# Order of the first loads, of the first two weight conversions and of the down-weight sums in a retention + SwiGLU kernel

## The chip, the cores and the metric

One core of one Trainium2 chip. The metric is the device time of one execution in microseconds, the median of several runs. A time is compared only with runs of the kernel before that were made on the same chip at the same time. Ratios are the mean time of one kernel's fast runs over that of the other's of the same rounds, so they are not quite the ratio of the medians quoted beside them.

The engines have short names in the profile: PE is TensorE, DVE is VectorE, ACT is ScalarE, POOL is GpSimd, SP is the engine that issues the loads.

## The reference

```python
# retention: B, H, S, D = 4, 8, 768, 64
for t in range(S):
    state = gamma * state + outer(k[:, :, t], v[:, :, t])
    y[:, :, t] = scale * (q[:, :, t] @ state)
# feed-forward: x is (3072, 512), d_ff = 1536; the three weights are 64-bit floats
g = x @ w_gate
out = (g * sigmoid(g) * (x @ w_val)) @ w_out
```

## The kernel before

The work goes in four segments of 768 tokens. Attention of a segment is done in six chunks of 128 positions, then twelve "up" blocks f = 0 to 11 compute the hidden activations, then a "down" stage multiplies by w_out, interleaved with the attention of the next segment. Up and down products use a scheme with seven products in place of eight, which needs sums of weights and sums of activations (`xs`, `hs`).

The first segment is special. The weights arrive as 64-bit words and are converted on the chip to 32-bit, piece by piece, while the blocks run. Twelve "up" pieces and six "down" pieces go through three steps and then their sums. The line numbers are those that the profile of the kernel before shows:

```python
def convert_a(piece):                                   # ScalarE, L172 and L173
    nc.scalar.activation(d, hi, AF.Abs)
    nc.scalar.activation(lo, lo, AF.Copy, scale=2.0 ** -51, bias=2.0)
def convert_b(piece):                                   # VectorE, L179 and L181
    nc.vector.tensor_scalar(d, d, ...min, max)
    nc.vector.tensor_scalar(hi, hi, 0x80000000, None, op0=ALU.bitwise_and)
def convert_c(piece):
    nc.vector.scalar_tensor_tensor(u, u, 3, hi, ...)    # VectorE, L188
    nc.gpsimd.tensor_tensor(d, u, lo, op=ALU.add)       # GpSimd, L190, "the add"
def sums_t(piece):                                      # L201 to L203
    sub = (nc.gpsimd if kind == "up" else nc.vector).tensor_tensor
    sub(both, ...); sub(w[:, T2], ...); sub(w[:, T4], ...)
```

An up block, with its calls into the conversion (cut):

```python
def up(s, f, convert):
    product(x, B11, a_up(0, 0));  nc.scalar.copy(p1, x)          # L359
    product(wb, T1, s1);          nc.scalar.copy(p5, wb)         # L362
    ...                                # Silu of the block before, ScalarE
    convert(f, 0)                      # b and c of the next-but-one pieces
    product(x, T2, s2, start=False);  nc.scalar.copy(u2, x)      # L368
    product(wb, B22, s4, start=False); tt(hT[:, f, 0], wb, u2)   # VectorE, L370
    product(x, T3, s3, start=False);   tt(hT[:, f, 1], x, p5)    # VectorE, L372
    ...                                # gate products of the block before, L389, L390
    convert(f, 1)
    product(z, B21, a_up(0, 1));       tt(c11, z, p1)            # VectorE, L380
    product(x, T4, a_up(1, 1), start=False)   # adds into x: must wait for L372
```

The traces show VectorE taking its instructions in program order: where the down sums (L201, at 111.67) wait 2.51 us for GpSimd, all that follows them waits too. The last product adds into `x`, which L372 has to read first; so whatever stands before L372 in VectorE's order can hold up TensorE.

Of the kernel before, what the change touches and what calls it, by code (L numbers as in the profile page):

```python
# [32 lines left out]
MASK0, QDEC0, KDEC0, GDEC0 = 0, 2 * NP * P, 3 * NP * P, 3 * NP * P + H  # L33
# [4 lines left out]
def tile_retnet_swiglu(  # L38
# [32 lines left out]
    nc = tc.nc  # L71
# [10 lines left out]
    first = early.__enter__()  # L82
# [4 lines left out]
    def bank(tag, bufs, name):  # L87
        return psum.tile([P, 512], F32, tag=tag, name=name, bufs=bufs)


    chunks = {}

    def load_chunk(c, pool, tag, between=lambda nm: None):
        tiles = []
        for nm, src in (("kt", k_t), ("qt", q_t), ("vn", v_n), ("kn", k_n)):
            t = pool.tile([P, 512], F32, tag=nm + tag, name=f"{nm}_{c}")
            nc.sync.dma_start(out=t, in_=src[c])
            tiles.append(t)
            between(nm)
        chunks[c] = tiles  # L100

    def seg_chunks(s):

        p, pos = divmod(s * L, NCK)
        return [(2 * p + i) * NCK + pos + j for j in range(L) for i in range(2)]

    tab = consts.tile([P, NTAB], F32, name="tab")
# [17 lines left out]
    def load_piece(piece):  # L125


        kind, a = piece
        to = new_wt(0, a) if kind == "up" else wot[a]
        if kind == "up":  # L130
            halves = [w[:, ts(a, P)].rearrange("(c p) f -> p c f", p=P)
                      for w in (w_gate, w_val)]
            parts = [(halves[1][:, ds(KH, KH)], B22), (halves[1][:, ds(0, KH)], B12),
                     (halves[0], B11)]
        else:
            top, low = (w_out[ts(a + FH * i, P)] for i in range(2))
            parts = [(low[:, DH:], B22), (top[:, DH:], B12), (top[:, :DH], B11),
                     (low[:, :DH], B21)]
        if w_gate.dtype != F32:
            raw[piece] = raws.tile([P, 4, 2 * KH * P], U32, tag="raw",  # L140
                                   name=f"raw_{kind}{a}")
        for src, slot in parts:
            if w_gate.dtype == F32:
                t = to[:, slot:]
            else:
                t, src = raw[piece][:, slot - B22:], src.bitcast(U32)
            if len(src.shape) == 3:
                c, f = src.shape[1:]
                t = t.rearrange("p a b -> p (a b)")[:, : c * f]
                t = t.rearrange("p (c f) -> p c f", c=c)  # L150
            else:
                t = t[:, 0]
            nc.sync.dma_start(out=t, in_=src)
# [8 lines left out]
    def words_of(piece):  # L162
        kind, a = piece
        w = wt[0, a] if kind == "up" else wot[a]
        d = w[:, ds(B22, 4)].rearrange("p a b -> p (a b)")
        r = raw[piece].rearrange("p a (n two) -> p (a n) two", two=2)
        return w, d, r[:, :, 0], r[:, :, 1]

    def convert_a(piece):
        if piece in raw:  # L170
            w, d, lo, hi = words_of(piece)
            nc.scalar.activation(d, hi.bitcast(F32), AF.Abs)  # L172
            nc.scalar.activation(lo.bitcast(F32), lo, AF.Copy, scale=2.0 ** -51,  # L173
                                 bias=2.0)

    def convert_b(piece):
        if piece in raw:
            w, d, lo, hi = words_of(piece)
            nc.vector.tensor_scalar(d, d, 122879.9921875, 2.0 ** -15, op0=ALU.min,  # L179
                                    op1=ALU.max)  # L180
            nc.vector.tensor_scalar(hi, hi, 0x80000000, None, op0=ALU.bitwise_and)  # L181
# [12 lines left out]
    def sums_t(piece):  # L194
        kind, a = piece
        w = wt[0, a] if kind == "up" else wot[a]
        sub = (nc.gpsimd if kind == "up" else nc.vector).tensor_tensor
        flat = w.rearrange("p a b -> p (a b)")
        n = KH * P
        both = flat[:, : 4 * n].rearrange("p (a b) -> p a b", b=2 * n)[:, :, :n]  # L200
        sub(both, w[:, ds(B22, 2)], w[:, ds(B12, 2)], op=ALU.subtract)  # L201
        sub(w[:, T2], w[:, B22], w[:, T1], op=ALU.subtract)
        sub(w[:, T4], w[:, B21], w[:, T2], op=ALU.subtract)  # L203
        if kind == "up":
            nc.sync.dma_start(out=wstore[a], in_=w)
# [8 lines left out]
    def load_next():  # L214
        if to_load:
            load_piece(to_load.pop(0))
# [107 lines left out]
    def a_up(i, j):  # L324
        return xT[:, ds(KH * j, KH), i]
# [13 lines left out]
    late = []  # L339

    def up(s, f, convert):
        w = wt.pop((s, f)).rearrange("p o (k f) -> p o k f", k=KH)
        s1, s2, s3, s4 = xs
        x = bank("x", 2, f"x_{s}_{f}")[:, :TH]
        wb = bank("wz", 2, f"w_{s}_{f}")[:, :TH]

        def product(o, slot, a, start=True, stop=True):
            for k in range(KH):
                nc.tensor.matmul(o, w[:, slot, k], a[:, k], start=(start and k == 0),  # L349
                                 stop=(stop and k == KH - 1), skip_group_check=True)  # L350

        def tmp(nm, bufs):
            return io.tile([P, TH], F32, tag=nm, name=f"{nm}_{s}_{f}", bufs=bufs)

        add, mul = ALU.add, ALU.mult
        tt = nc.vector.tensor_tensor
        product(x, B11, a_up(0, 0))
        p1 = tmp("p1", 2)
        nc.scalar.copy(p1, x)  # L359
        product(wb, T1, s1)  # L360
        p5 = tmp("p5", 1)
        nc.scalar.copy(p5, wb)  # L362
        if late:
            late[0]()
        convert(f, 0)
        product(x, T2, s2, start=False)
        u2 = tmp("u2", 1)
        nc.scalar.copy(u2, x)  # L368
        product(wb, B22, s4, start=False)
        tt(hT[:, f, 0], wb, u2, op=add)  # L370
        product(x, T3, s3, start=False)
        tt(hT[:, f, 1], x, p5, op=add)  # L372
        if late:
            late.pop(0)
            late.pop(0)()
        convert(f, 1)
        z = bank("wz", 2, f"z_{s}_{f}")[:, :TH]
        product(z, B21, a_up(0, 1))
        c11 = tmp("c11", 2)
        tt(c11, z, p1, op=add)  # L380
        product(x, T4, a_up(1, 1), start=False)
        sg = tmp("sg", 1)

        def gates():
            nc.scalar.activation(c11, c11, AF.Silu)
            nc.scalar.activation(sg, x, AF.Silu)

        def muls():
            tt(hT[:, f, 0], hT[:, f, 0], c11, op=mul)  # L389
            tt(hT[:, f, 1], hT[:, f, 1], sg, op=mul)  # L390

        late.extend([gates, muls])
# [63 lines left out]
            nc.scalar.dma_start(out=out[ds(row, P)], in_=ev[i])  # L456


    def table(nm):
        if nm == "qt":  # L460
            nc.sync.dma_start(out=tab[:, :QDEC0], in_=decays[:, :QDEC0])
        elif nm == "vn":
            nc.sync.dma_start(out=tab[:, QDEC0:], in_=decays[:, QDEC0:])

    cs = seg_chunks(0)
    load_chunk(cs[0], first, "0", table)
    for n in range(1, len(cs)):
        load_chunk(cs[n], first, str(n))
        if n in (1, 3, 4):
            load_next()  # L470
    steps = retention(0)

    def retain(k):
        for _ in range(k):
            if steps:
                steps.pop(0)()

    u0, u1 = order[:2]
    retain(3)
    convert_a(u0)  # L480
    retain(3)
    convert_b(u0)
    retain(2)
    convert_c(u0)
    load_next()
    convert_a(u1)
    retain(3)
    convert_b(u1)
    retain(1)
    sums_t(u0)  # L490
    retain(4)
    convert_c(u1)
    load_next()
    retain(len(steps))
# [3 lines left out]
    due = [u1]  # L498
# [3 lines left out]
    def convert(f, part):  # L502
        now = at_block[f]
        if part == 0:
            while due:
                sums_t(due.pop(0))
            for p in now:
                convert_b(p)
            for p in now[:1]:
                convert_c(p)  # L510
                load_next()
                if p[0] == "up":
                    sums_t(p)
                else:
                    due.append(p)
        else:
            for p in now[1:]:
                convert_c(p)
                load_next()
                due.append(p)  # L520
            for p in at_block[f + 1] if f + 1 < NF else []:
                convert_a(p)

    for s in range(NSEG):
        nxt = seg_chunks(s + 1) if s + 1 < NSEG else []
# [70 lines left out]
```

## Time and profile before

| | before |
|---|---|
| median of 4 runs (range) | 795.73 us (794.53 to 796.8) |
| TensorE busy | 758.9 us, 96% |
| TensorE's largest wait | 13.9 us, for L372 on VectorE |
| two up blocks, first segment / later segments | 22.5 us / 18.06 us |

A line of a wait list reads: who waited, for whom, us in total, times, longest. A line of the order of time reads: start in us, duration in us, engine, line, operation, output<-inputs, form, and in brackets the idle time before it and what ended it. The lines themselves are shown in the prediction.

### The profile page before, as it was taken

Reading aid. Unit: us, or ns where it says so; the run is one execution under the profiler, and the core shown is the slowest. Engines: PE = TensorE matmul, PEld = TensorE weight load, DVE = VectorE, ACT = ScalarE, POOL = GpSimd, SP = SyncE. Lnnn points to the kernel's source line nnn. Section 1 sums busy time; section 2 is a strip of 40 time slices with the busy share of each in tenths; the row PEclk is TensorE's granted clock in tenths of the full one; section 3 lists DMA queues with packets and bytes.
Section 4 is the critical chain, followed back from the end, with each engine's and each line's share of the span. In section 5 each row is a group of like instructions: output and inputs, shape, how many; then the busy total and the mean of one; then the engine's idle time right before and its main releaser. Section 6 shows DMA issues by size and latency. Waiting matters only on the chain.

```text
span 794.6 us, 8792 instructions
## 1 busy us (share of the span) xinstructions
PE 758.9 (96%) x3440; PEld 532.4 (67%) x3440; DVE 333.4 (42%) x524; ACT 202.4 (25%) x422; POOL 138.2 (17%) x102
## 2 busy tenths in 40 slices
PE   5889888989999999999999999999999999999997
PEld 4755454557888555557888655556888755555886
DVE  2778888885241232225441322225433222223520
ACT  2374454411211222221122222322111122322100
POOL 3665766732110000100211000001211000000000
PEclk9899999999999999999999999999999999999999
DMA  9856667331550223500532223320254023310010
GB/s 328 287 199 232 203 220 250 148 120 54 186 195 31 93 92 99 192 0 28 199 118 108 73 93 113 128 97 14 67 212 159 27 93 113 119 47 0 1 54 26
DMA packets 40840, 95.73 MB, mean 120 GB/s; under 512 B 3680, under 2 KB 15968, under 8 KB 40800
## 3 DMA queue, kind: packets, MB, share of 16 engines
q1 hardware_dynamic: 37344, 88.89, 32.1%
q10 hardware_dynamic: 3456, 6.29, 2.3%
q8 instruction: 27, 0.44, 0.2%
q14 instruction: 13, 0.11, 0.0%
HBM read 77.86 MB, written 17.30 MB: 120 GB/s over the span
## 4 chain that ended last, share of the span: by engine, by line
PE 77%; DVE 3%; issue 0%; ACT 0%; DVEq 0%; ACTq 0%
PE x L349 24%; PE dx L417 15%; PE w L349 12%; PE dw L417 7%; PE z L349 6%; PE dz L417 4%; PE y L296 2%; PE s L246 2%; PE y L292 2%; PE st L274 2%; DVE hs L407 1%; DVE hT L390 0%; DVE a L251 0%; DVE hT L372 0%; DVE wot L201 0%
## 5 line engine op out<-in xcount | busy, mean ns | idle before, releaser
L349 PE MATMUL x<-xT,wt 128*128 128x384 f32 x384 | 136.3, 497 | 13.9 <-DVE hT L372 13.9
L349 PE MATMUL x<-xs,wt 128*128 128x384 f32 x384 | 139.8, 487 | 1.2 <-ACT u L368 1.2
L349 PE MATMUL w<-xs,wt 128*128 128x384 f32 x384 | 139.6, 486 | 0.9 <-DVE xs L334 0.9
L349 PEld LDWEIGHTS x<-xT,wt 128*128 128x128 f32 x384 | 73.8, 194 | 67.6 <-issue 20.8
L370 DVE TENSOR_TENSOR hT<-w,u 128x384 f32<-128x384 f32 x48 | 26.7, 557 | 214.0 <-PE w L349 213.1
L349 PEld LDWEIGHTS x<-xs,wt 128*128 128x128 f32 x384 | 72.7, 190 | 53.2 <-ACT u L368 3.3
L349 PEld LDWEIGHTS w<-xs,wt 128*128 128x128 f32 x384 | 73.0, 190 | 52.4 <-DVE xs L334 1.6
L257 POOL TENSOR_TENSOR kn<-kn,tab 128x512 f32<-128x512 f32 x20 | 25.2, 1261 | 330.4 <-DMA kn<-in_k_n_dram 330.4
L359 ACT COPY p<-x 128x384 f32<-128x384 f32 x48 | 23.0, 479 | 226.2 <-PE x L349 226.1
L349 PE MATMUL z<-xT,wt 128*128 128x384 f32 x192 | 69.8, 486 | 0.0
L417 PE MATMUL dw<-wot,hs 128*128 128x256 f32 x288 | 67.3, 383 | 0.0
L417 PE MATMUL dx<-wot,hs 128*128 128x256 f32 x288 | 67.0, 382 | 0.0
L417 PE MATMUL dx<-wot,hT 128*128 128x256 f32 x288 | 66.4, 381 | 0.0
L417 PEld LDWEIGHTS dw<-wot,hs 128*128 128x128 f32 x288 | 53.7, 190 | 8.7 <-issue 1.5
L417 PEld LDWEIGHTS dx<-wot,hT 128*128 128x128 f32 x288 | 53.7, 190 | 8.7 <-issue 0.9
L417 PEld LDWEIGHTS dx<-wot,hs 128*128 128x128 f32 x288 | 53.4, 190 | 7.7
L349 PEld LDWEIGHTS z<-xT,wt 128*128 128x128 f32 x192 | 36.5, 190 | 25.4
L299 ACT COPY xT<-y 128x512 f32<-128x512 f32 x24 | 14.1, 587 | 149.7 <-PE y L296 149.7
L251 DVE TENSOR_TENSOR a<-s,tab 128x512 f32<-128x512 f32 x48 | 30.9, 684 | 44.8 <-PE s L246 44.8
L281 DVE TENSOR_TENSOR state<-state,st 64x256 f32<-64x256 f32 x32 | 13.4, 419 | 79.8 <-PE st L274 77.1
L246 PE MATMUL s<-qt,kt 64*128 64x128 f32 x384 | 30.7, 298 | 12.8 <-DMA qt<-in_q_t_dram 10.5
L260 POOL TENSOR_TENSOR qt<-qt,tab 128x512 f32<-128x512 f32 x20 | 26.6, 1331 | 91.2 <-PE s L246 56.3
(58 smaller groups left out, 774.0 us busy)
## 6 DMA issues: line engine op xcount, KB each, us to landing
wt<-wstore SPq DMA_DIRECT2D x36, 896.0 KB, 4.6
wstore<-wt SPq DMA_DIRECT2D x12, 896.0 KB, 4.4
kt<-in_k_t_dram SPq DMA_DIRECT2D x24, 256.0 KB, 4.8
qt<-in_q_t_dram SPq DMA_DIRECT2D x24, 256.0 KB, 3.3
vn<-in_v_n_dram SPq DMA_DIRECT2D x24, 256.0 KB, 4.8
kn<-in_k_n_dram SPq DMA_DIRECT2D x24, 256.0 KB, 5.1
raw_up<-in_w_val_dram SPq DMA_DIRECT2D x24, 256.0 KB, 3.1
raw_up<-in_w_gate_dram SPq DMA_DIRECT2D x12, 512.0 KB, 5.0
```

The source lines that it names most:

```text
L246: nc.tensor.matmul(sp[i][:, ts(n, P)], kt[r, n], qt[r, n], start=True, stop=True, skip_group_check=True)
L251: nc.vector.tensor_tensor(t, pairs(sp[i]), mask[:, i], op=ALU.mult)
L257: nc.gpsimd.tensor_tensor(kd, kd, kdec[:, :, None].to_broadcast([P, H, D]), op=ALU.mult)
L260: nc.gpsimd.tensor_tensor(qt, qt, qdec, op=ALU.mult)
L274: nc.tensor.matmul(st[:, ts(n, P)], kd[:, ts(n, P)], vn[:, ts(n, P)], start=(n == 0), stop=True, skip_group_check=True)
L292: nc.tensor.matmul(y[:, ts(n, P)], prev[:, n], qd[:, n], start=(n == 0), stop=False, skip_group_check=True)
L296: nc.tensor.matmul(y[ds(D * i, D), ts(n, P)], vn[:, ts(2 * n + i, D)], a[i][:, n], start=(ci == 0 and n == 0), stop=True, skip_group_check ...
L299: nc.scalar.copy(xT[:, :, c // NCK % 2, ts(ci % L, P)], pairs(y))
L349: nc.tensor.matmul(o, w[:, slot, k], a[:, k], start=(start and k == 0), stop=(stop and k == KH - 1), skip_group_check=True)
L359: nc.scalar.copy(p1, x)
L370: tt(hT[:, f, 0], wb, u2, op=add)
L417: nc.tensor.matmul(o, a[:, k], wot[k][:, slot], start=(start and k == 0), stop=(k == FH - 1), skip_group_check=True)
```

## The change

The intent: let attention start with less of the load queue ahead of it, keep weight conversions out of its way, and keep VectorE from waiting for GpSimd's add of a down piece at the head of a block. The core of the diff, cut and condensed (several calls on one line):

```diff
-    load_chunk(cs[0], first, "0", table)
-    for n in range(1, len(cs)):
+    load_chunk(cs[0], first, "0", ("kt", "qt"));  # table, first part
+    load_chunk(cs[1], first, "1", ("kt", "qt"))
+    load_chunk(cs[0], first, "0", ("vn", "kn"));  # table, rest
+    load_chunk(cs[1], first, "1", ("vn", "kn"))
+    for n in range(2, len(cs)):
         load_chunk(cs[n], first, str(n))
-        if n in (1, 3, 4):
+        if n in (2, 4, 5):
             load_next()                # a weight piece
```
```diff
-    retain(3); convert_a(u0); retain(3); convert_b(u0); retain(2); convert_c(u0)
-    load_next()
-    convert_a(u1); retain(3); convert_b(u1); retain(1); sums_t(u0)
-    retain(4); convert_c(u1); load_next()
+    retain(9); convert_a(u0); retain(2); convert_b(u0); retain(1); convert_c(u0)
+    load_next()
+    retain(4); sums_t(u0); convert_a(u1)
+    retain(4); convert_b(u1); convert_c(u1); load_next()
     retain(len(steps))
```
```diff
     def convert(f, part):
         if part == 0:
-            while due:
-                sums_t(due.pop(0))
+            for p in [p for p in due if p[0] == "up"]:
+                sums_t(p); due.remove(p)
 ...
+        else:                          # part 2, new: called after L380 of the block
+            while due:
+                sums_t(due.pop(0))
+            due.extend(p for p in now if p[0] == "down")
```

`retain(k)` runs the next k steps of attention (scores, mix and state update of a chunk, and after every two chunks the sums `xs`, called x sums below). The step of the scores ends with VectorE's mask product (L251: scores times the decay mask) and with GpSimd's scaling of k and q (L257, L260). `u0` and `u1` are the first two up pieces, the first and second weight of the prediction. The x sums of chunks three and four stand ahead of the sixth chunk's scores and mask product in both kernels; what the second diff moves behind the last state update is the whole VectorE conversion of `u1`.

More of the change, by code (lines that the diff above doesn't have):

```diff
@@ L91, in tile_retnet_swiglu, with load_chunk @@
     chunks = {}
-    def load_chunk(c, pool, tag, between=lambda nm: None):
-        tiles = []
-        for nm, src in (("kt", k_t), ("qt", q_t), ("vn", v_n), ("kn", k_n)):
+    def load_chunk(c, pool, tag, names=("kt", "qt", "vn", "kn")):
+        for nm in names:
             t = pool.tile([P, 512], F32, tag=nm + tag, name=f"{nm}_{c}")
+            src = {"kt": k_t, "qt": q_t, "vn": v_n, "kn": k_n}[nm]
             nc.sync.dma_start(out=t, in_=src[c])
-            tiles.append(t)
-            between(nm)
-        chunks[c] = tiles
+            chunks.setdefault(c, []).append(t)
     def seg_chunks(s):
@@ L380, in up @@
         tt(c11, z, p1, op=add)
+        convert(f, 2)
         product(x, T4, a_up(1, 1), start=False)
@@ L456, in down @@
             nc.scalar.dma_start(out=out[ds(row, P)], in_=ev[i])
-    def table(nm):
-        if nm == "qt":
-            nc.sync.dma_start(out=tab[:, :QDEC0], in_=decays[:, :QDEC0])
-        elif nm == "vn":
-            nc.sync.dma_start(out=tab[:, QDEC0:], in_=decays[:, QDEC0:])
-    cs = seg_chunks(0)
-    load_chunk(cs[0], first, "0", table)
-    for n in range(1, len(cs)):
+    cs = seg_chunks(0)
+    early_parts = [("kt", "qt"), ("vn", "kn")]
+    load_chunk(cs[0], first, "0", early_parts[0])
+    nc.sync.dma_start(out=tab[:, :QDEC0], in_=decays[:, :QDEC0])
+    load_chunk(cs[1], first, "1", early_parts[0])
+    load_chunk(cs[0], first, "0", early_parts[1])
+    nc.sync.dma_start(out=tab[:, QDEC0:], in_=decays[:, QDEC0:])
+    load_chunk(cs[1], first, "1", early_parts[1])
+    for n in range(2, len(cs)):
         load_chunk(cs[n], first, str(n))
-        if n in (1, 3, 4):
+        if n in (2, 4, 5):
             load_next()
@@ L478, in tile_retnet_swiglu @@
     u0, u1 = order[:2]
-    retain(3)
+    retain(9)
     convert_a(u0)
-    retain(3)
+    retain(2)
     convert_b(u0)
-    retain(2)
+    retain(1)
     convert_c(u0)
     load_next()
+    retain(4)
+    sums_t(u0)
     convert_a(u1)
-    retain(3)
+    retain(4)
     convert_b(u1)
-    retain(1)
-    sums_t(u0)
-    retain(4)
     convert_c(u1)
@@ L504, in convert @@
         if part == 0:
-            while due:
-                sums_t(due.pop(0))
+            for p in [p for p in due if p[0] == "up"]:
+                sums_t(p)
+                due.remove(p)
             for p in now:
@@ L513, in convert @@
                     sums_t(p)
-                else:
-                    due.append(p)
-        else:
+        elif part == 1:
             for p in now[1:]:
@@ L519, in convert @@
                 load_next()
-                due.append(p)
             for p in at_block[f + 1] if f + 1 < NF else []:
                 convert_a(p)
+        else:
+            while due:
+                sums_t(due.pop(0))
+            due.extend(p for p in now if p[0] == "down")
     for s in range(NSEG):
```

## The prediction

> **What bounds the kernel now.** I read the page first, then who waits for whom on TensorE, then the order of time in two places. The page says that TensorE is the engine to watch, and the list of its waits says where it stands still.
>
> ```profile
> PE 758.9 (96%) x3440; PEld 532.4 (67%) x3440; DVE 333.4 (42%) x524; ACT 202.4 (25%) x422; POOL 138.2 (17%) x102
> ...
> DVE  2778888885241232225441322225433222223520
> POOL 3665766732110000100211000001211000000000
> ```
>
> ```profile
> PE x L349 <- DVE hT L372: 13.9, 5, 3.5
> PE s L246 <- DMA qt<-in_q_t_dram: 10.5, 4, 4.7
> ```
>
> Both waits lie in the first 170 us: the opening (six attention chunks, loaded from HBM, up to 41.8 us) and the first segment's twelve "up" blocks, in which the 64-bit weight words are converted. In later segments a block takes 9.03 us (chain of work: the same pair of products starts at 288.02 and 297.05), which is TensorE alone. Here two blocks take 22.5 us on average: L372 ends at 71.69 in block 2 and at 161.67 in block 10, so (161.67 - 71.69) / 4. Hence the twelve blocks lose some 20 us to something else. One even block shows what:
>
> ```profile
> 106.94 1.74 DVE L188 SCALAR_TENSOR_TENSOR wot<-wot,raw_down 128x1024 uint32<-128x1024 uint32 x1
> 107.68 1.59 POOL L203 TENSOR_TENSOR wt<-wt 128x256 f32<-128x256 f32 x1
> 109.24 2.40 POOL L190 TENSOR_TENSOR wot<-wot,raw_down 128x1024 int32<-128x1024 int32 x1
> 111.67 0.69 DVE L201 TENSOR_TENSOR wot<-wot 128x512 f32<-128x512 f32 x1 [2.51 <-POOL wot L190]
> ...
> 114.52 1.23 DVE L188 SCALAR_TENSOR_TENSOR wt<-wt,raw_up 128x1024 uint32<-128x1024 uint32 x1
> 115.66 0.55 DVE L370 TENSOR_TENSOR hT<-w,u 128x384 f32<-128x384 f32 x1
> 115.96 2.40 POOL L190 TENSOR_TENSOR wt<-wt,raw_up 128x1024 int32<-128x1024 int32 x1 [4.33 <-DMA raw_down<-in_w_out_dram]
> 116.13 0.55 DVE L372 TENSOR_TENSOR hT<-x,p 128x384 f32<-128x384 f32 x1
> 116.59 2.18 DVE L389 TENSOR_TENSOR hT<-hT,c 128x384 f32<-128x384 f32 x1
> 116.82 2.82 PE L349 MATMUL x<-xT,wt 128*128 128x384 f32 x8 [2.50 <-DVE hT L372]
> ```
>
> VectorE works in order. The down sums (L201) wait 2.51 us for GpSimd's add, then the next weight's conversion runs, then L372, and TensorE waits for that. The reader should also see the lengths. L389 takes 0.55 us in later segments and 2.18 here: it ends 0.41 after GpSimd's add (115.96 + 2.40 = 118.36). L203 on GpSimd takes 0.72 alone and 1.59 here, behind L188. The two engines are taking turns.
>
> **What the Trainium skill says.** "SBUF — State Buffer", section "Who interferes with whom": VectorE operations with two SBUF inputs, and tensor_scalar in its two-port mode, share a port with GpSimd; whoever comes first has it for the whole instruction and the other is blocked. The trace agrees: the lengths above fit no other way, and L370 and L372, which read PSUM, keep their 0.55 us beside GpSimd's add. "TensorE: Matmul & The Clock Gate", section "What's actually happening": the clock halves after an idle window of about 3.4 us. The trace agrees: after two of the five waits (3.46 us each, at 94 and 139 us) eight products take 4.51 instead of 2.74 us.
>
> **The change, part by part.**
>
> *Down sums moved.* They leave the head of a block for its end, after L380, one block section later. No instruction is removed. VectorE loses the 2.51 us of waiting, and the sums' 1.5 us leave the path to L372 of an even block. The tempting sum is 13.9 us of waits plus two cold stretches of 1.8 us, 17 us in all. I don't take it, because the port is full. Its bill for two blocks (three weights, one of them a down weight), with each operation at its length without waiting:
> - GpSimd: three adds of 2.4 and two sets of up sums of 1.27 + 0.73 + 0.72: 12.6 us.
> - VectorE: six L179/L181 of 0.6, three L188 of 1.1, four gate products of 0.41, down sums 1.1: 9.6 us.
>
> Together 22.2 us, against the 22.5 measured and TensorE's 18.06. So I play the order through by hand with the rule "who waits gets the port when the other ends". Let a be the time by which the up add ends after L372 ends in an odd block. Then the gate products, GpSimd's sums and L188 of the down weight alternate to a + 3.65, the last sum ends at a + 4.24. Before: the down add ends at a + 6.6, then the sums, L179, L181, L188: L372 of the even block ends at a + 11.6 (measured 12.1 with a = 0.47, 13.3 with a = 1.7). After: L179 takes the port first, the down add ends at a + 7.04, L181 and L188 at a + 8.7, L372 at a + 9.65. The sums then lie before the odd block's two conversions: from the even block's L372 to the odd one's 9.0 + a', a' = 1.6 being the same delay in the even block, so 10.6 instead of 9.2 to 10.4. With a = 1.5 two blocks take 11.2 + 10.6 = 21.8 us. Saving: 0.7 us per two blocks, and 1.5 once, in block 2, where the sums first go.
>
> *Loads and first conversions.* Before, the sixth chunk comes after the third weight; now before it. The rate in the opening is about 370 GB/s, by the DMA view of the first 60 us. The first weight, now after three chunks and the table (5 MB), should land at 17 us, the second at 25.4, the sixth chunk's k at 28.4 instead of near 31. This is worth something to attention, which no longer stands behind conversions at 18 to 28 us: scores of chunk six would run at 27.7 instead of 33.80. But then VectorE has the four sums of L334 to L337 ahead of the sixth mask product, just when GpSimd runs the first weight's add, the k and q scalings (1.04, 1.27) and that weight's sums: each sum waits for one of them. I get the mask product at 35.5 instead of 37.55, and the last state update (L281) at 40.0 to 40.5 instead of 42.07.
>
> ```profile
> 37.55 1.29 DVE L251 TENSOR_TENSOR a<-s,tab 128x512 f32<-128x512 f32 x2
> 38.76 1.22 DVE L188 SCALAR_TENSOR_TENSOR wt<-wt,raw_up 128x1024 uint32<-128x1024 uint32 x1
> ...
> 40.10 2.40 POOL L190 TENSOR_TENSOR wt<-wt,raw_up 128x1024 int32<-128x1024 int32 x1 [3.66 <-DVE wt L188]
> ...
> 42.07 0.85 DVE L281 TENSOR_TENSOR state<-state,st 64x256 f32<-64x256 f32 x2 [1.34 <-PE st L274]
> ...
> 42.94 1.21 DVE L334 TENSOR_TENSOR xs<-xT 128x256 f32<-128x256 f32 x1
> ```
>
> In this stretch the second weight's L188 and add (38.76 and 40.10) stand before the last state update. After the change its whole VectorE conversion (2.4 us) and its add (2.4 us) stand behind it, on a full port, and ahead of the last x sums. So 4.8 us are added there, and 2.0 to 2.4 come off: the conversions in the blocks start about 2.4 us later (third weight's L188 ends near 51.1, not 48.7). The first block's opening product can start at 39 instead of 41.80, but its second product still waits for L334 near 43.3, and TensorE may stand 3 us there.
>
> *Sum.* Start of the blocks' conversions: +2.4. Block 1 of the kernel before waits for TensorE and ScalarE (its L372 starts at 59.58, with the port's work ahead of it done), which takes up 1.1 of this, so +1.3 at the first down weight's L188; the moved sums take off 1.5 at L372 of block 2: -0.2 there. Four more pairs of blocks at -0.7: -2.9, thus -3.1 at block 10. The last block is bound by TensorE in both (8.7 us), so it keeps this. Then the last down sums (1.5 us) fall between L380 of block 11 and the last gate products, partly under ScalarE's Silu; those products end 2.5 us after L380 instead of 1.6: +0.9, which the first products of the down stage feel, as VectorE's sums of hT and the next mask product already make TensorE wait there. Total -2.2 us: 795.3 - 2.2 = 793.1, say 793.
>
> **The rivals.**
> 1. *The waits simply go.* L372 is on time, TensorE runs at 9.03 us a block, 13 to 17 us are saved, 779 to 783 us. For: TensorE is busy 96%, and the wait named is the largest. Against: the port's bill, which no move of an instruction shrinks.
> 2. *GpSimd falls behind and catches up in blocks 10 and 11*, which convert little. VectorE, no longer tied to the down add, would follow TensorE more closely. At most one to two weights of lag, 3 to 6 us, 787 to 790. Against: three raw buffers; the down weight's load waits for the add of the down weight before it.
> 3. *That load takes the wait's place.* It lands 5.6 to 6.0 us after the add, and ScalarE's convert of it (2.3 us) stands before the copy of the next block's first product. I get this copy at 5.4 us after the even block's L372, where TensorE would want it at 2.7; TensorE loses 2 us but only up to 0.1 beyond what VectorE makes it wait. If loads are 1 us slower it costs 4 to 5 us over the stage: 797.
> 4. *The opening gains more* (5 us, if the x sums do not meet GpSimd's work) or loses more: 788 or 796.
>
> **Range and chances.** The middle is 793; rivals 2 and 4 pull down by up to 5 us, 3 and 4 up by up to 4. Eight in ten: 788 to 797. Faster by over 2% needs under 779.4 us, that is rival 1 in full: 0.03. Slower by over 2%: 0.01. Within 2%: 0.96.
>
> **What would show it.** Right: the wait of TensorE for L372 is not gone but spread over odd and even blocks, each under 3 us, without cold products; two blocks take 21.5 to 22; "DVE wot L201 <- POOL wot L190" is gone from the waits; gate products stay near 2 us long; the second weight's add ends near 46 instead of 42.5. Wrong: two blocks near 18 to 20 us (the port is not the limit), the first L372 earlier than the 49.66 of before (the opening gained), or a new wait of TensorE for the copy L359 that sets L372.

## The result, and the profile after

| | before | changed |
|---|---|---|
| median (range), 4 runs each | 795.73 us (794.53 to 796.8) | 800.29 us (798.92 to 801.12) |
| ratio, 95% interval | | 1.0056 (1.0035 to 1.0077) |
| span of the profiled run | 794.6 us | 799.3 us |

The changed kernel is 0.56% slower, where 793 us was predicted and 788 to 797 as range. Line numbers below are two less than before (L370 is the old L372, L186 the old L188, L188 the old L190, L199 the old L201, L332 to L335 the old L334 to L337), and one less behind the new call: L388 is the old L389, L416 the old L417.

The list of TensorE's waits in the changed kernel answers the first question, whether the wait at L372 went:

```profile
PE x L347 <- DVE hT L370: 7.9, 7, 1.6
PE x L347 <- ACT p L357: 4.9, 4, 1.5
PE w L347 <- DVE xs L332: 2.7, 1, 2.7
```

It fell from 13.9 to 7.9 us, in seven waits instead of five, and beside it stand waits for the copy L357 (4.9 us, none of that kind before) and for the x sums (2.7, was 0.9). The same even block as in the prediction, in order of time in the changed kernel:

```profile
111.06 1.74 DVE L186 SCALAR_TENSOR_TENSOR wot<-wot,raw_down 128x1024 uint32<-128x1024 uint32 x1
...
113.19 0.74 DVE L177 TENSOR_SCALAR wt<-wt 128x1024 f32<-128x1024 f32 x1
...
113.35 2.83 POOL L188 TENSOR_TENSOR wot<-wot,raw_down 128x1024 int32<-128x1024 int32 x1
...
113.86 2.88 DVE L179 TENSOR_SCALAR raw_up<-raw_up 128x1024 uint32<-128x1024 uint32 x1
...
116.77 1.23 DVE L186 SCALAR_TENSOR_TENSOR wt<-wt,raw_up 128x1024 uint32<-128x1024 uint32 x1
...
118.39 0.54 DVE L370 TENSOR_TENSOR hT<-x,p 128x384 f32<-128x384 f32 x1
```

The sums no longer stand here. But L179, 0.69 us when alone, now takes 2.88, because it stands behind the same add. VectorE waits inside an instruction in place of in front of one. The busy time of each engine between 100 and 164 us (columns: window, its length, then busy us and instructions of PE, PEld, DVE, ACT, POOL, granted clock, DMA share, GB/s), before:

```profile
100.00:164.00 64.00, 55.24 (x164) 31.31 (x163) 54.08 (x64) 28.27 (x43) 40.28 (x24) 0.97 0.53 189
```

and changed:

```profile
100.00:164.00 64.00, 54.61 (x163) 29.83 (x162) 63.69 (x66) 29.59 (x46) 43.10 (x27) 1.00 0.56 201
```

VectorE goes from 54.08 to 63.69 us of 64: it never stops, and the records of its instructions hold the time in which GpSimd has the port. TensorE does no more than before.

The opening in the changed kernel:

```profile
31.53 2.03 DVE L332 TENSOR_TENSOR xs<-xT 128x256 f32<-128x256 f32 x1
...
37.58 1.29 DVE L249 TENSOR_TENSOR a<-s,tab 128x512 f32<-128x512 f32 x2
...
38.93 1.80 PE L294 MATMUL y<-a,vn 128*64 128x128 f32 x14 [0.17 <-DVE a L249]
...
40.66 2.05 PE L272 MATMUL st<-vn,kn 128*128 128x128 f32 x8
...
42.82 0.85 DVE L279 TENSOR_TENSOR state<-state,st 64x256 f32<-64x256 f32 x2 [3.19 <-PE st L272]
...
45.01 1.23 DVE L186 SCALAR_TENSOR_TENSOR wt<-wt,raw_up 128x1024 uint32<-128x1024 uint32 x1
...
46.37 2.45 POOL L188 TENSOR_TENSOR wt<-wt,raw_up 128x1024 int32<-128x1024 int32 x1 [7.43 <-DVE wt L186]
...
46.72 1.53 PE L347 MATMUL w<-xs,wt 128*128 128x384 f32 x4 [2.72 <-DVE xs L332]
```

The mask product at 37.58 is no earlier than before (37.55). The products behind it run on a slow TensorE clock: fourteen take 1.80 us, where sixteen of the kind take 1.09 on the full clock, and eight of st take 2.05 in place of 1.13 to 1.16. The second piece's add ends at 48.82, in the kernel before at 42.50.

How far the changed kernel is behind (+) at the same point of the work, from the starts and ends in the two traces:

| point | before | changed | difference | predicted |
|---|---|---|---|---|
| third weight's L188 (old number) ends | 48.69 | 54.40 | +5.7 | +2.4 |
| L372 (old number) of block 2 ends | 71.69 | 74.89 | +3.2 | -0.2 |
| L372 of block 10 ends | 161.67 | 162.99 | +1.3 | -3.1 |
| first product of the down stage starts | 172.21 | 173.53 | +1.3 | -3.1 |
| second weight-sum product (dw) there starts | 187.01 | 191.92 | +4.9 | -2.2 |

So the changed kernel is 3.2 us behind at block 2 (the opening's loss, less what the moved sums take off there), the blocks win back 1.9, and the first down stage loses 3.6. That last loss, before:

```profile
175.99 2.86 PE L417 MATMUL dw<-wot,hs 128*128 128x256 f32 x12
...
180.62 1.75 PE L246 MATMUL s<-qt,kt 64*128 64x128 f32 x16 [1.78 <-DVE a L251]
182.31 2.86 PE L417 MATMUL dx<-wot,hs 128*128 128x256 f32 x12
```

and changed:

```profile
173.76 0.67 DVE L199 TENSOR_TENSOR wot<-wot 128x512 f32<-128x512 f32 x1
...
177.34 2.86 PE L416 MATMUL dw<-wot,hs 128*128 128x256 f32 x12
...
182.59 2.67 PE L244 MATMUL s<-qt,kt 64*128 64x128 f32 x16 [2.39 <-DVE a L249]
...
185.19 4.88 PE L416 MATMUL dx<-wot,hs 128*128 128x256 f32 x12
```

The last down sums (L199, at 173.76) now delay VectorE's sums of hT and the next mask product. TensorE waits 2.39 us in place of 1.78, and after that wait its clock is low: sixteen products take 2.67 in place of 1.75, twelve take 4.88 in place of 2.86. The record of the granted clock says the same: 0.50 from 182.59 to 185.19 and 0.56 from 185.19 to 189.90, against 1.00 before (180.62 to 187.00). The wait costs 0.6 us and the clock 2.9.

### The profile page after: what moved, and what is told of

Read it like the earlier page. It is cut to its first block, busy times and chain, and to the rows that moved or that the text cites. A ratio compares the mean times of both kernels' runs of the same rounds, so it can differ in the third digit from the quotient of the medians.

```text
span 799.3 us, 8795 instructions
## 1 busy us (share of the span) xinstructions
PE 762.3 (95%) x3440; PEld 533.7 (67%) x3440; DVE 351.1 (44%) x524; ACT 201.6 (25%) x422; POOL 141.3 (18%) x102
## 4 chain that ended last, share of the span: by engine, by line
PE 79%; DVE 14%; issue 3%; DMA 3%; ACT 1%; POOL 0%; SPq 0%; DVEq 0%; ACTq 0%; POOLq 0%
PE x L347 24%; PE dx L416 16%; PE w L347 12%; PE dw L416 7%; PE z L347 6%; PE dz L416 4%; PE y L294 3%; PE s L244 3%; PE y L290 2%; PE st L272 2%; DVE raw_up L179 2%; DVE hT L389 2%; DVE hT L388 2%; DVE hs L406 1%; DVE wot L186 1%
## 5 line engine op out<-in xcount | busy, mean ns | idle before, releaser
L347 PE MATMUL x<-xT,wt 128*128 128x384 f32 x384 | 132.9, 488 | 7.9 <-DVE hT L370 7.9
L357 ACT COPY p<-x 128x384 f32<-128x384 f32 x48 | 22.9, 477 | 224.5 <-PE x L347 224.5
L416 PE MATMUL dx<-wot,hs 128*128 128x256 f32 x288 | 69.1, 391 | 0.0
L416 PE MATMUL dw<-wot,hs 128*128 128x256 f32 x288 | 67.3, 383 | 0.0
L416 PE MATMUL dx<-wot,hT 128*128 128x256 f32 x288 | 66.4, 381 | 0.0
L416 PEld LDWEIGHTS dx<-wot,hs 128*128 128x128 f32 x288 | 54.9, 195 | 8.4 <-issue 0.2
L416 PEld LDWEIGHTS dw<-wot,hs 128*128 128x128 f32 x288 | 53.7, 190 | 8.8 <-issue 1.5
L416 PEld LDWEIGHTS dx<-wot,hT 128*128 128x128 f32 x288 | 53.7, 190 | 8.6 <-issue 1.0
L244 PE MATMUL s<-qt,kt 64*128 64x128 f32 x384 | 33.1, 311 | 11.6 <-DMA qt<-in_q_t_dram 8.6
```

Of the source, the lines that this page charges most:

```text
L244: nc.tensor.matmul(sp[i][:, ts(n, P)], kt[r, n], qt[r, n], start=True, stop=True, skip_group_check=True)
L347: nc.tensor.matmul(o, w[:, slot, k], a[:, k], start=(start and k == 0), stop=(stop and k == KH - 1), skip_group_check=True)
L416: nc.tensor.matmul(o, a[:, k], wot[k][:, slot], start=(start and k == 0), stop=(k == FH - 1), skip_group_check=True)
```

## The experiments

Eleven kernels ran, in three sets, each set on one chip beside eleven runs of the kernel before (median 796.35, 796.45 and 796.68 us). All gave correct results. "Stretch" is the time from the first product of the first down stage to the second dw product, 14.80 us before and 18.39 in the first profile of the changed kernel.

**e1_sums_only**: the kernel before with the third diff alone.

> The kernel before with only the down sums moved. Theory (port): the two-block period falls from 22.5 to about 22.0 and block 2 is 1.6 us earlier, so the last block is some 3.4 us earlier than before; the last down sums, ahead of the sums of hT, then give back 0.65 us of waiting, and a cold TensorE clock may add 2.9 as in the changed kernel: 792.6 us without the cold stretch, 795.5 with it. Rival (the move itself is what costs): 797 or more. Rival (the waits simply go): 782.

Measured: 794.23 us, ratio 0.9971 (0.9959 to 0.9984). L372 of block 2 ends at 69.98 and of block 10 at 158.05, 3.6 us earlier than before; two blocks take (158.05 - 69.98) / 4 = 22.02 us. TensorE waits 2.09 us for the mask product and twelve products after it take 4.42 us; the stretch is 16.75. The port theory holds, and so does the loss at the end. Both rivals fall.

**e6_sums_only_last_early**: the same, but the last down piece's sums stay at the head of block 11, where VectorE has nothing else to do.

```diff
-            for p in [p for p in due if p[0] == "up"]:
+            for p in [p for p in due if p[0] == "up" or f == NF - 1]:
```

> The kernel before with the down sums moved, except the last one. Theory: keeps the 3.4 us won in the blocks and has neither the longer wait nor the cold stretch: 792.3 us, faster than both kernels. Rival: no different from moving all of them.

Measured: 791.53 us, 0.9947 (0.9932 to 0.9963). The stretch is 13.45 us, without a slow product. As expected; this is faster than both kernels.

**e5_after_last_sums_early**: the same edit in the changed kernel.

> The changed kernel, but the last down weight's sums (block 11) stay at the head of the block, where VectorE is idle. Theory: the wait for the mask product in the down stage goes back from 2.4 to 1.8 us and the cold stretch behind it goes: 3.5 us less, 796.8 us. Rival (the cold stretch is chance, or comes from elsewhere): 0.6 us less, 799.7.

Measured: 795.38 us, 0.9993 (0.9978 to 1.0008). The stretch is 13.31 us:

```profile
176.04 2.86 PE L416 MATMUL dw<-wot,hs 128*128 128x256 f32 x12
...
179.18 1.75 PE L244 MATMUL s<-qt,kt 64*128 64x128 f32 x16 [0.29 <-DVE a L249]
180.87 2.86 PE L416 MATMUL dx<-wot,hs 128*128 128x256 f32 x12
```

The wait goes to 0.29 us, lower than the 1.8 expected, and the slow products go. So 1.5 us of sums in the wrong place cost the changed kernel 3.6 to 5 us, by the ratios of its two measurements (1.0038 in e12, 1.0056 first) to this one. The stretch is also 1.5 us shorter than in the profiled run of the kernel before, which I had not expected. It is 13.30 to 13.50 in all nine experiments that keep the last sums at the head of block 11 (e2 to e8, e10, e11): there VectorE's third sum of hT gets to the port before GpSimd's scaling of q. In the profiled run of the kernel before it came 0.11 us after, and the stretch was 14.80. So up to 1.5 us of any gain over the kernel before in these nine comes from this order and not from the edit tried. That run is the median of its eleven (796.35 us); without the 1.5 us it would be near 794.9, by this estimate, which is below the fastest of them (795.06). This suggests that the kernel before loses the 1.5 us as a rule, but only one execution of it was profiled.

**e4_loads_and_conv**: the first two diffs without the third.

> The changed order of loads and of the first conversions, with the down sums as before. Theory: the opening alone costs 4 to 5 us at the start of the down stage, two blocks still take 22.5 us, TensorE's wait for the mask product in the down stage is 1.8 us as before and no stretch is cold: 799.5 to 800.5 us. Rival (the sums are what costs, the opening is neutral): 795 to 796.

Measured: 798.41 us, 1.0030 (1.0018 to 1.0042). L372 of block 2 ends at 75.17 (+3.5), of block 10 at 165.16 (+3.5), two blocks 22.5 us. The opening costs what the theory says at block 2; TensorE's wait for the mask product is 0.48 us, not the 1.8 expected, and the stretch of 13.5 us gives 1.3 back, so the total is 1 to 2 us under what was expected.

**e2_loads_only** and **e3_conv_only**: the first diff alone, the second alone.

> The kernel before with only the new order of loads. Theory: the first weight lands later, and ScalarE and VectorE wait for it ahead of attention's work, but the x sums do not stand before the sixth mask product beside a full GpSimd; opening neutral within 2 us: 795 to 798 us. Rival (the loads are what costs the 4 us of the opening): 799 to 801.

> The kernel before with only the new order of the first two conversions. Theory (this order costs: x sums ahead of the sixth mask product, the whole second conversion behind the last state update): start of the blocks 3 to 5 us later, 799 to 801 us. Rival (the loads cost): 796 or less.

Measured: loads only 797.18 us, 1.0002 (0.9990 to 1.0014); conversions only 799.75 us, 1.0041 (1.0028 to 1.0054). L372 of block 0 ends at 50.88 with the loads and at 54.26 with the conversions, against 50.22 before. The order of the conversions makes nearly the whole loss of the opening. The new order of the loads is neutral in the total, but its profile shows parts that cancel: 0.6 to 0.7 us behind at blocks 0, 2 and 10, 2.3 behind at block 11 (after a wait of 3.44 us, eight products take 4.51 us in place of 2.82), and 1.5 back in the stretch of 13.30.

**e7_mask_before_xsums**: e5 with the scores and mask product of the sixth chunk ahead of the second x sums.

```diff
     steps = retention(0)
+    steps[14], steps[15] = steps[15], steps[14]
```

> The changed kernel with the last down sums early, and the sixth chunk's scores and mask product ahead of the second x sums. Theory (the mask product stood behind four sums that each waited for one GpSimd operation, and TensorE cooled down meanwhile): the last state update ends about 3.5 us earlier, and the blocks keep it: 3 us less than without the swap, 792.5 us. Rival (the opening is set by the loads or by the conversion alone): under 1 us less, 795.

Measured: 794.33 us, 0.9963 (0.9948 to 0.9978), 0.3% better than e5 by the ratios, 2.4 us (the two intervals just touch). The mask product starts at 29.46 in place of 36.18, but the last state update only at 39.06 in place of 41.60: TensorE then waits 1.91 us for GpSimd's scaling of q, which now takes turns with the x sums. The gain expected there was 3.5; it was 2.5.

**e11_second_conv_earlier**: e7 with VectorE's conversion of the second piece ahead of the last state update.

```diff
-    retain(4); convert_b(u1); convert_c(u1)
+    retain(2); convert_b(u1); convert_c(u1); retain(2)
```

> The changed kernel with the last down sums early, the sixth mask product first, and VectorE's conversion of the second weight ahead of the last state update, in the 2.8 us in which VectorE idles there. Theory (the conversion behind the last state update is what delays the blocks): the second weight's add ends 3.5 to 4 us earlier, the blocks start 2 to 2.5 us earlier and stay so: 792 us or less, level with the best so far. Rival (the rest of the opening sets it): within 1 us of the version without this, 794.

Measured: 791.96 us, 0.9938 (0.9924 to 0.9952), by the ratios 2 us better than e7, though the intervals overlap a little. Its profiled run reached the first piece's L186 some 2.3 us later than e7's, so I compare from there: from the end of that L186 to the end of L370 in block 0 it takes 24.9 us in e5, 23.0 in e7 and 20.1 in e11. This names two things. The loss against the kernel before is mostly the second conversion behind the last state update: from the end of that update to the end of the third weight's L188 it was 5.77 us before and is 10.73 in the changed kernel, 5.0 of the 5.7 us in the table. The x sums ahead of the mask product are a gain not made: with them the mask product comes no earlier than before (37.58 and 37.55; 37.39 in e3).

**e8_spare_adds**: the kernel before with a useless GpSimd addition behind each down piece's add, at a place where GpSimd sits idle for over 4 us and nobody reads the result.

```diff
+            if kind == "down":
+                nc.gpsimd.tensor_tensor(spare, tab[:, :512], tab[:, 512:1024], op=ALU.add)
```

> The kernel before with six spare GpSimd additions of 128x512 (about 1.1 us each), one behind each down weight's add, where GpSimd would sit idle for over 4 us; nobody waits for their result. Port theory (VectorE's sums and conversion run then and take turns with it): each costs about 1 us, 5 to 6 us more: 801 us. Rival (GpSimd has idle time to spare): within 1 us of before.

Measured: 801.58 us, 1.0062 (1.0050 to 1.0074). From block 4 to block 10 two blocks take (167.16 - 96.52) / 3 = 23.55 us, in the kernel before (161.67 - 94.18) / 3 = 22.50: each spare addition costs 1.05 us although its engine had time. Its line, and the down sum beside it:

```profile
111.56 2.38 POOL L191 TENSOR_TENSOR wot<-wot,raw_down 128x1024 int32<-128x1024 int32 x1
113.91 1.28 POOL L194 TENSOR_TENSOR spare<-tab 128x512 f32<-128x512 f32 x1
113.97 1.76 DVE L205 TENSOR_TENSOR wot<-wot 128x512 f32<-128x512 f32 x1 [2.50 <-POOL wot L191]
```

L205, 0.69 us when alone, ends 0.54 after the spare addition does. That is the port, shown by itself.

**e12_changed_again**: the changed kernel once more.

> The changed kernel once more, unaltered, beside the versions below on one chip. Theory: 4 to 5 us over before again (800.5 us), in its profile 18.4 us from the first product of the first down stage to the second weight product, against 13.3 where the last sums stay early. Rival (the long down stage of the first profile was chance): 13 to 15 us there and a time near 797.

Measured: 800.16 us, 1.0038 (1.0026 to 1.0051). The stretch was 16.42 us, not 18.4: TensorE waits 1.78 us for the mask product, and behind it sixteen products take 2.33 and twelve 3.91 us. So the slow clock comes again, but what it costs differs from run to run, between 1.6 and 2.9 us. The parts do not add up to the whole: e4 and e1 multiplied give a ratio of 1.0001, the changed kernel measured 1.0056 and 1.0038. In the profiles the rest lies in the stretch (e12 16.42, first profile 18.39; e4's 13.5 and the 2.0 that e1 added would make 15.5) and in the opening, where L372 of block 0 ended at 54.99 and 55.45 against 53.89 in e4, with the same code up to there. No edit explains this rest.

**e10_sums_mask_first**: e6 with the swap of e7, in the old order of loads and conversions.

> The kernel before with the down sums moved except the last, and the sixth mask product ahead of the second x sums, in the old order of loads and conversions. Theory: the last state update comes about 1.4 us earlier, but the second weight's conversion is where it was, so the full port of the blocks starts no earlier: at most 1 us less than the same without the swap, 791 us. Rival (attention sets the start of the blocks): 1.5 to 3 us less, 789.

Measured: 790.82 us, 0.9929 (0.9916 to 0.9942), the fastest. L372 of block 0 ends at 49.73, in e6 at 50.05. The theory holds: a quicker attention gains little where the second piece's conversion stays in its place. Against e6 the intervals overlap.

## Why the prediction was wrong

*The port is full, so the waits do not simply go: right.* 22.2 us of port time per two blocks were counted, 21.8 us predicted as the new pace, 22.02 and 22.03 measured (e1 and the changed kernel). The bill was thus slightly too high, as a pace below it shows (and the predicted 21.8 already contradicted it). e8 shows the port apart from everything else; that the lengths "fit no other way" was until then only argued. Over four pairs this is 1.9 us won where 2.9 were predicted, an error of 1.0. The relations of the working held: in block 6 the up add ends a = 1.68 us after the L370 before it, and L370 of the even block ends 11.43 us after that one, against a + 9.65 = 11.33. But a was put at 1.5, as GpSimd's add starts 0.22 us after L186 ends (118.22 and 118.00 in the block shown) and I had counted about half of that.

*The start of the blocks' conversions at +2.4: wrong in size, and this is the largest single error.* It measured +5.7, and at block 2 the difference was +3.2 in place of -0.2: an error of 3.4 us that the blocks then carry along. Direction and place were right: x sums in front of the mask product, the second conversion behind the last state update (e3, e7, e11). The 4.8 us added behind that update were right too: they measured 5.0 (10.73 less 5.77). What failed is the credit of 2.0 to 2.4 us for an earlier state update. Two terms of it were too small. The mask product was put at 35.5 and came at 37.58. In e5, with the same code up to there, it came at 36.18, and the sixth scores at 27.66, where the prediction had 27.7; the other 1.4 us are a difference between two runs of the same code: in the changed kernel's profile the fourth chunk's scores met a slow clock (sixteen products in 2.08 us from 18.77 on, 1.16 in e5). And the products between mask product and state update were counted at the full clock; after TensorE had stood still twice (1.90 and 1.25 us by the list of its waits) they took 1.8 to 2.1 us in place of 1.1 each. So the last state update started at 42.82 (41.60 in e5), not at 40.0 to 40.5: against 42.07 before, the credit was a debit of 0.75 us.

*The last down sums at +0.9: the step that failed outright.* The prediction had the place (the sums of hT and the next mask product) and the delay itself: the gate products end 2.45 us after L380 of block 11, 1.62 before, where 2.5 and 1.6 were named. It had nothing of what TensorE makes of this delay. The first down stage measured +3.6. Of this the longer wait is 0.6; the rest is the low clock after a wait of 2.39 us. The prediction had even cited the clock for the blocks, and then counted no cold product anywhere in the changed kernel. e5 and e6 show that moving these sums back removes both. Against the 13.3 to 13.5 us of the nine profiles with the sums in place, the loss is 3.3 (e1), 3.1 (e12) and 5.1 us (the first profile), so the +3.6 owes part of its size to the 14.80 of the one profile before.

*The sum.* 3.4 + 1.0 + 2.7 (that is 3.6 less 0.9) = 7.1 us, and the median is 800.3 where the sum gave 793.1.

*The rivals.* The first (13 to 17 us saved) is refuted. The third appeared: TensorE waits 4.9 us for the copy L357 behind the convert of a down piece. But it did not set the pace: VectorE, which releases TensorE next, ran without a pause in the same stretch (63.69 of 64 us). Of the second nothing was seen: the last block takes 8.72 us in both. Of the fourth, the losing side came true. Of the signs that I had named, these came: waits at L370 of at most 1.6 us without slow products in the blocks, no wait of the down sums for the add, gate products at 2.17 us. The wait at L370 did not spread as named: six of its seven times are in even blocks, the one in an odd block is 0.39 us; what the odd blocks lose shows at the copy L357. The second piece's add ended at 48.82 where "near 46" was named.

What stays open: whether the kernel before loses the 1.3 to 1.5 us of its profiled down stage in every execution, why the changed kernel loses more than its parts, and how much of the loss on TensorE's clock, in the opening and in the down stage, is chance from run to run.

## What to carry to other kernels

Before counting a wait as a gain, add up what the engines on both sides need of what they share: here VectorE and GpSimd together filled their port, so a removed wait came back as longer instructions. An order that delays a chain while TensorE has nothing else to do can be paid twice, once as the wait and once as slow products after it (0.6 and 2.9 us here); so sums that nobody needs yet belong where their engine is idle, not just behind something else. And parts of a change should be tried apart: here one of three won 0.5% with a one-line repair, one was neutral, and one lost 0.4%.

## What the Trainium skill lacked or had wrong

- "SBUF — State Buffer", section "Who interferes with whom", says that whoever comes first has the port and the other is blocked. It does not say who gets it next when both queues are full: here the lengths fit the rule that the one that waits gets it when the other ends, so that the two alternate instruction by instruction (by this rule an even block was to take 11.33 us and took 11.43; a gate product of 0.55 us takes 2.17, the L179 of 0.69 takes 2.88, a spare addition costs 1.05 us of time on an engine that idles 4 us). It gives no way to see a full port in a profile; in the changed kernel it was VectorE busy 63.69 of 64 us, but in the kernel before, at 54.08, a spare addition cost 1.05 us as well.
- "TensorE: Matmul & The Clock Gate", section "What's actually happening", has the clock fall after an idle window of about 3.4 us. Here it was low after single waits of 1.78 us (e12: twelve products in 3.91 us, granted clock 0.71), 2.09 us (e1: 4.42, 0.62) and 2.39 us (4.88, 0.56), against 2.86 us at 1.00, while waits of 1.78 us (twelve in 2.86) and of 2.50 us (the eight products in 2.82 us in the prediction's lines) left it high in the kernel before. A wait well under the named window can thus be enough, and need not be.
- "Perfetto Trace Analysis", section "GPSIMD Engine Instruction", calls GpSimd's recorded spans unreliable. Here they held: the add took 2.38 to 2.45 us wherever VectorE left it alone, and the blocked VectorE instructions read here ended 0.41 to 0.56 us after the recorded end of GpSimd's.
